# Attention and a feed-forward product on one core: later q and k loaded in 128-byte rows and transposed by VectorE, and the first block's weight operands requested by ScalarE

## The chip, the cores and the metric

One core of a Trainium2 chip. The time is device microseconds (us) of one execution, the median of several. The kernel before took 1540.1 us (three runs, 1538.55 to 1542.52; 1540.2 with a fourth, which ran beside the result); in the later series on two chips its medians were 1538.6 to 1539.1. "Faster" and "slower" mean by more than 2%. Ratios are the mean time of one kernel's runs over that of the kernel before's runs of the same rounds, so they are not quite the ratio of the medians that stand beside them. Stage lengths and waits come from one profiled run of each kernel.

## The reference, cut to what matters

```python
# q, k, v: (8, 12, 448, 64) float32;  w_in: (768, 2048), w_out: (2048, 768), both float64
q_n, k_n = rmsnorm(q, g_q), rmsnorm(k, g_k)          # over the 64 columns
attn = softmax(q_n @ k_n.T / 8)
x = (attn @ v) -> (8 * 448, 12 * 64)
h = maximum(x @ w_in, 0);  out = (h * h) @ w_out
```

Of the kernel before, what the change touches and what calls it, by code (L numbers as in the profile page):

```python
# [303 lines left out]
def load_pair(nc, qk, q, k, i):  # L304

    _, H, S, D = q.shape
    b, h0 = divmod(2 * i, H)
    for dst, src in ((qk[:, 0], q), (qk[:, 1], k)):
        nc.sync.dma_start(dst, src[b, h0:h0 + 2].rearrange("h (p j) d -> p h (j d)", j=4))
# [3 lines left out]
def attention_then_ffn_bounded(  # L313
# [48 lines left out]
    NSPAN = B // 2  # L362
    assert 2 * D == P and S % NJ == 0 and SP <= P and B % 2 == 0 and NPAIR % 2 == 0 and NFC % 2 == 0
# [4 lines left out]
    small = ctx.enter_context(tc.tile_pool(name="small", bufs=4))  # L368
# [8 lines left out]
    mhalf = consts.tile([SP, 2 * 2 * NJ], F32, name="mhalf")  # L377
    qk1 = consts.tile([SP, 2, 2, NJ * D], F32, name="qk1")
# [170 lines left out]
    def load_blocks(upto):  # L549

        while len(stream) < min(upto, NSPAN * (N1 + N2)):
            n = len(stream) % (N1 + N2)
            if written[0] < min(2 * (n // 7 + 1) if n < N1 else 2 * NFC, 2 * NFC):
                return
            sw = loads.tile([P, 4, P], F32, tag="sw", name="sw", bufs=5)
            if n < N1:
                sw = sw[:, 0:HC]
                src = w1s[n // 7, n % 7]
            else:
                n -= N1  # L560
                src = w2s[*uses2[n // (HF // 4)], n % (HF // 4)]
            nc.sync.dma_start(sw.rearrange("p c m -> p (c m)"), src)
            stream.append(sw)
# [5 lines left out]
    def load(i):  # L569
        qks[i] = (qk0, qk1)[i % 2]  # L570
        load_pair(nc, qks[i], q, k, i)

    def load_v(i):
        b, h0 = i // NPAIR, 2 * (i % NPAIR)
        vs[i] = loads.tile([SP, 2, NJ, D], F32, tag="vt", name="vt")
        nc.sync.dma_start(vs[i].rearrange("p h j d -> p h (j d)"),
                          v[b, h0:h0 + 2].rearrange("h (p j) d -> p h (j d)", j=NJ))

    def norm(i):
        qk = qks.pop(i)  # L580
        qkn = loads.tile([SP, 2, NJ, 2, D], F32, tag="qkn", name="qkn", bufs=2)
        sq = qkn.rearrange("p s j h d -> p (s j h d)")
        flat = qk.rearrange("p s h e -> p (s h e)")
        nc.scalar.activation(sq, flat, AF.Square)
# [4 lines left out]
        nc.gpsimd.tensor_tensor(rflat, rflat, mhalf, ALU.pow)  # L589
# [8 lines left out]
    def transposes(i, alone=False):  # L598
        qkn = normed.pop(i)
        if alone:  # L600
            pts[i] = [ps_m.tile([P, S], F32, tag="m", name="pt") for _ in range(2)]
        else:
            pt = ps_s.tile([P, 2, 512], F32, tag="s", name="pts")
            pts[i] = [pt[:, s, 0:S] for s in range(2)]
        for s, pt in enumerate(pts[i]):
            for j in range(NJ):
                nc.tensor.transpose(pt[:, j * SP:(j + 1) * SP],  # L607
                                    qkn[:, s, j].rearrange("p h d -> p (h d)"), ident[:SP, :SP])

    def take_transposes(i):  # L610
        qkTs[i] = loads.tile([P, 2, S], F32, tag="qkT", name="qkT")
        for s, pt in enumerate(pts.pop(i)):
            nc.scalar.activation(qkTs[i][:, s], pt, AF.Copy, scale=gains[:, s:s + 1])  # L613
# [37 lines left out]
    def finish(work, i):  # L651

        b, hp = divmod(i, NPAIR)
        rec = work.tile([P, S], F32, tag="rec", name="rec", bufs=1)
        nc.vector.reciprocal(rec, tots.pop(i))  # L655
        nc.vector.tensor_tensor(xT[:, b % 2, hp].rearrange("d (p j) -> d j p", j=NJ),
                                pavs.pop(i).rearrange("d (j p) -> d j p", j=NJ),
                                rec.rearrange("d (j p) -> d j p", j=NJ), ALU.mult)
        del vs[i]
# [15 lines left out]
    def attention(work, first, end, alone):  # L675


        last = (first // (2 * NPAIR) + 1) * 2 * NPAIR
        for i in range(first, end):
            if i + 3 < min(last + 2, B * NPAIR):  # L680
                load(i + 3)
            scores(work, i, 0, alone)
            scores(work, i, 1, alone)
            if i + 2 < last:
                norm(i + 2)
# [6 lines left out]
            if alone and i + 1 < last:  # L692
                transposes(i + 1, True)
            scores(work, i, 2, alone)
            scores(work, i, 3, alone)
            if alone:
                if i + 1 < last:
                    take_transposes(i + 1)
                yield
            values(i, alone)  # L700
            finish(work, i)
            if i == end - 1:
                combine_x(i)
            if not alone:
                if i + 1 < last:
                    transposes(i + 1)
                    take_transposes(i + 1)
# [142 lines left out]
    nc.vector.tensor_scalar(gains[:, 0:1], gains[:, 0:1], float(D) ** -0.5, None, ALU.mult)  # L850

    ALONE = 2

    def start_of(span):
        return 2 * span * NPAIR

    def ahead(u, nxt):
# [6 lines left out]
        if u == 7 * (HF - 1):  # L864
            transposes(nxt)
            take_transposes(nxt)

    with tc.tile_pool(name="words", bufs=2) as spare["pool"]:
# [5 lines left out]
        transposes(0, True)  # L874
# [4 lines left out]
        with tc.tile_pool(name="first_product", bufs=2, reuse_waits="tile") as work:  # L879
            for u, _ in enumerate(first_product(work, 0)):  # L880
                weights(EARLY + (LATE - EARLY) * (u + 1) // N1)
                ahead(u, start_of(1))
        with tc.tile_pool(name="alone", bufs=2, reuse_waits="tile") as work:
            for u, _ in enumerate(attention(work, start_of(1), start_of(1) + ALONE, True)):
                weights(LATE + (ALL - LATE) * (u + 1) // ALONE)
# [23 lines left out]
def kernel(  # L909
# [22 lines left out]
    qk0 = bound.tile([q.shape[2] // 4, 2, 2, 4 * D], F32, name="qk0")  # L932
# [48 lines left out]
```

## The kernel before: the parts that the change and the argument touch

Work goes by **head pairs** (two heads of a batch, 48 pairs) and by **spans** (two batches, 12 pairs, four spans). "Span" in this sense is a block of work; the span of a profile is the whole execution. The products are done by a seven-product scheme on half blocks; its weight operands are prepared on the chip in span 0 from the float64 words, written to device memory (`w1s`, `w2s`) and streamed back as `sw`. The order of the stages is: attention of span 0 with the weights' preparation beside it; first product of span 0 (the rest of the preparation beside it); two **lone pairs** (12 and 13) of span 1; then **mixed stages**, in which attention of the next span and the second product of the present one take turns on TensorE (PE), with first products of the later spans between them.

```python
def norm(i):                                  # one pair: 112 partitions x (q,k) x 2 heads x 4 rows x 64
    nc.scalar.activation(sq, flat, AF.Square)
    nc.vector.tensor_reduce(rflat, sq..., ALU.add)
    nc.vector.tensor_scalar(rflat, rflat, 1.0 / D, 1e-6, ALU.mult, ALU.add)
    nc.gpsimd.tensor_tensor(rflat, rflat, mhalf, ALU.pow)             # 16 columns
    for s in range(2):
        nc.gpsimd.tensor_tensor(qkn[:, s]..., qk[:, s]..., rstd..., ALU.mult)

def transposes(i, alone=False):               # PE, 8 per pair, into PSUM
    ...
            nc.tensor.transpose(pt[:, j * SP:(j + 1) * SP], qkn[:, s, j]..., ident[:SP, :SP])

def take_transposes(i):
    for s, pt in enumerate(pts.pop(i)):
        nc.scalar.activation(qkTs[i][:, s], pt, AF.Copy, scale=gains[:, s:s + 1])

def scores(work, i, c, pe_sums): ...          # sc = k.T q on PE; pr = exp(sc) on ScalarE; acc += pr on VectorE
def values(i, pe_sums): ...                   # pav = v.T pr on PE, then tot = ones.T acc on PE
def finish(work, i):
    nc.vector.reciprocal(rec, tots.pop(i))
    nc.vector.tensor_tensor(xT[...], pavs.pop(i)..., rec..., ALU.mult)

def attention(work, first, end, alone):       # alone: no second product beside it
    for i in range(first, end):
        ...load(i + 3); scores(i, 0); scores(i, 1); norm(i + 2)
        if not alone: yield                   # here the second product gets its turn
        ...scores(i, 2); scores(i, 3)
        if alone: ...; yield                  # here the weights' preparation gets its turn
        values(i, alone)
        finish(work, i)
        if not alone:
            if i + 1 < last:
                transposes(i + 1)
                take_transposes(i + 1)
            yield

def load_blocks(upto):                        # weight operands, five buffers
    ...
            nc.sync.dma_start(sw.rearrange("p c m -> p (c m)"), src)
```

## Time and profile before

| | before |
|---|---|
| median | 1540.1 us |
| span of the profiled run | 1535.9 us |
| PE busy | 1466.5 us, 95% |
| granted PE clock | 0.991 |
| PE starts the first product of span 0 | 157.2 us |
| PE starts the lone pairs | 311.7 us |
| PE starts the second product | 345.2 us |

The page's first part gives each engine's busy time and number of instructions; its second part cuts the span into 40 slices and gives busy tenths per slice. A group line reads: line of the kernel, engine, operation, output<-inputs, shapes, count | busy us, mean ns of one | idle us just before, with what ended it. A timeline line reads: start, duration, engine, line, operation, and in brackets how long the engine had been idle and what released it. A line of the waits reads: who waited <- for whom: us in total, times, longest. The lines themselves stand in the prediction.

### The profile page before, as it was taken

To read this page: it belongs to the slowest core of one execution; us is meant where nothing else is said; L and a number is where in the kernel's file an instruction comes from. 1 tells how busy PE (TensorE), PEld (TensorE's weight loads), DVE (VectorE), ACT (ScalarE), POOL (GpSimd) and SP (SyncE) were. 2 spreads that over 40 slices of the span, in tenths; PEclk is the share of its full clock that TensorE was granted. 3 is DMA by queue.
4 is the path that set the end of the run, shared out by engine and by line. 5 is a ranking of instruction groups with operands and counts; after the bars stand their busy time and mean duration, and the time that the engine had idled before them with its cause. 6 is when DMAs were issued, how large, how long until landed. Compare 5 with 4: busy or idle time off the path is not lost.

```text
span 1535.9 us, 14184 instructions
## 1 busy us (share of the span) xinstructions
PE 1466.5 (95%) x4968; PEld 681.0 (44%) x4968; DVE 808.5 (53%) x922; ACT 453.7 (30%) x622; POOL 517.4 (34%) x367
## 2 busy tenths in 40 slices
PE   5989888879999999999999999999999999999998
PEld 2433443424444445544444445554444445555554
DVE  3779987865765533345556642345556662332111
ACT  4766555542322201223322211123322221111000
POOL 4788567771322002433333102243333301221000
PEclk9999999999999999999999999999999999999999
DMA  5376786842333332333333333233324223333353
GB/s 160 96 212 191 256 287 228 276 146 79 96 90 103 91 93 87 88 115 97 72 102 89 89 86 97 88 100 92 96 83 104 71 71 99 88 88 101 102 112 74
DMA packets 224532, 180.36 MB, mean 117 GB/s; under 512 B 99012, under 2 KB 200900, under 8 KB 224452
## 3 DMA queue, kind: packets, MB, share of 16 engines
q1 hardware_dynamic: 224452, 179.36, 41.2%
q8 instruction: 42, 0.69, 0.2%
q14 instruction: 38, 0.31, 0.1%
HBM read 146.28 MB, written 33.03 MB: 117 GB/s over the span
## 4 chain that ended last, share of the span: by engine, by line
PE 74%; POOL 10%; DVE 7%; issue 5%; DMA 2%; ACT 1%; SPq 0%; POOLq 0%; DVEq 0%
PE ps L809 34%; PE pc L733 8%; PE pd L733 8%; PE pa L733 7%; PE sc L621 7%; DVE acc L629 5%; PE pb L733 4%; POOL rstd L589 3%; PE pav L638 3%; PE tot L649 2%; POOL qkn L591 2%; POOL gC L471 2%; PE pts L607 2%; POOL gC L478 1%; ACT pr L624 1%
## 5 line engine op out<-in xcount | busy, mean ns | idle before, releaser
L809 PE MATMUL ps<-gT,sw 128*128 128x448 f32 x768 | 302.2, 544 | 10.0 <-DMA sw<-w2s 10.0
L589 POOL TENSOR_TENSOR rstd<-rstd,mhalf 112x16 f32<-112x16 f32 x48 | 152.1, 3168 | 398.8 <-DVE rstd L588 398.8
L741 POOL TENSOR_TENSOR gT<-gT 128x448 f32<-128x448 f32 x112 | 112.9, 1008 | 454.5 <-ACT gT L737 454.0
L624 ACT ACTIVATE pr<-sc 112x896 f32<-112x896 f32 x192 | 166.1, 915 | 332.1 <-PE sc L621 331.8
L809 PE MATMUL ps<-gC,sw 128*128 128x448 f32 x576 | 227.1, 543 | 0.0
L809 PEld LDWEIGHTS ps<-gT,sw 128*128 128x128 f32 x768 | 143.6, 191 | 151.9 <-issue 140.5
L655 DVE RECIPROCAL rec<-tot 128x448 f32<-128x448 f32 x48 | 142.0, 2957 | 72.9 <-PE tot L649 72.9
L621 PE MATMUL sc<-qkT 64*112 64x448 f32 x768 | 172.6, 569 | 2.6 <-ACT qkT L613 1.6
L638 PE MATMUL pav<-pr,vt 112*64 112x448 f32 x768 | 163.1, 547 | 3.4 <-DMA vt<-in_v_dram 3.1
L733 PE MATMUL pa<-xT,sw 128*128 128x448 f32 x384 | 155.5, 541 | 0.2 <-DMA sw<-w1s 0.2
L809 PEld LDWEIGHTS ps<-gC,sw 128*128 128x128 f32 x576 | 106.9, 190 | 108.2 <-issue 105.5
L737 ACT ACTIVATE gT<-gT 128x448 f32<-128x448 f32 x96 | 55.2, 575 | 298.4 <-DVE gT L767 183.3
L629 DVE TENSOR_TENSOR acc<-acc,pr 112x896 f32<-112x896 f32 x68 | 96.8, 1423 | 86.9 <-ACT pr L624 83.3
L591 POOL TENSOR_TENSOR qkn<-qk,rstd 112x512 f32<-112x512 f32 x96 | 120.5, 1276 | 3.8
L621 PEld LDWEIGHTS sc<-qkT 64*112 64x112 f32 x768 | 61.9, 175 | 98.6 <-issue 90.0
L733 PEld LDWEIGHTS pa<-xT,sw 128*128 128x128 f32 x384 | 73.1, 191 | 73.1 <-issue 72.0
L638 PEld LDWEIGHTS pav<-pr,vt 112*64 112x64 f32 x768 | 51.7, 137 | 102.7 <-issue 84.0
L629 DVE TENSOR_TENSOR acc<-pr 112x896 f32<-112x896 f32 x34 | 37.1, 1091 | 102.9 <-ACT pr L624 102.9
L733 PE MATMUL pc<-xC,sw 128*128 128x448 f32 x192 | 79.2, 549 | 5.4 <-DMA sw<-w1s 5.4
L733 PE MATMUL pd<-xT,sw 128*128 128x448 f32 x192 | 79.1, 549 | 4.7 <-DVE z L756 4.7
L733 PE MATMUL pd<-xC,sw 128*128 128x448 f32 x192 | 77.8, 541 | 5.3 <-DVE gT L767 4.2
L733 PE MATMUL pb<-xC,sw 128*128 128x448 f32 x192 | 77.8, 540 | 3.3 <-DVE gC L483 1.6
(82 smaller groups left out, 1404.8 us busy)
## 6 DMA issues: line engine op xcount, KB each, us to landing
sw<-w1s SPq DMA_DIRECT2D x224, 192.0 KB, 2.4
sw<-w2s SPq DMA_DIRECT2D x168, 256.0 KB, 2.7
qk<-in_q_dram SPq DMA_DIRECT2D x48, 224.0 KB, 3.3
qk<-in_k_dram SPq DMA_DIRECT2D x48, 224.0 KB, 3.7
vt<-in_v_dram SPq DMA_DIRECT2D x48, 224.0 KB, 3.7
w1s<-gC SPq DMA_DIRECT2D x8, 1344.0 KB, 6.0
w2s<-gC SPq DMA_DIRECT2D x24, 448.0 KB, 3.7
out_dram<-osb SPq DMA_DIRECT2D x192, 56.0 KB, 1.9
```

The lines of the kernel that those rows point to most:

```text
L471: nc.gpsimd.tensor_tensor(b[to[n % 2][half]], f[:, part], e[:, part], ALU.mult)
L589: nc.gpsimd.tensor_tensor(rflat, rflat, mhalf, ALU.pow)
L591: nc.gpsimd.tensor_tensor(qkn[:, s].rearrange("p j h d -> p h j d"), qk[:, s].rearrange("p h (j d) -> p h j d", d=D), rstd[:, s].rearrange ...
L621: nc.tensor.matmul(sc[:, h, 0:S], qkT[rows, 1, c * SP:(c + 1) * SP], qkT[rows, 0, :], start=True, stop=True)
L624: nc.scalar.activation(pr, sc[:, :, 0:S], AF.Exp)
L629: nc.vector.tensor_tensor(accs[i], probs[i, 0] if c == 1 else accs[i], pr, ALU.add)
L638: nc.tensor.matmul(pavs[i][h * D:(h + 1) * D, :], vs[i][:, h, c, :], pr[:, h, :], start=(c == 0), stop=(c == NJ - 1))
L655: nc.vector.reciprocal(rec, tots.pop(i))
L733: nc.tensor.matmul(ps, stream[n][:, c], rhs[:, c], start=first and c == 0, stop=c == HC - 1, skip_group_check=not first)
L737: nc.scalar.activation(g, src, AF.Relu)
L741: nc.gpsimd.tensor_tensor(g, g, g, ALU.mult)
L809: nc.tensor.matmul(ps, stream[n][:, c % 4], rhs_of[i][:, c], start=c == 0, stop=c == HF - 1)
```

## The change

Its intent: take 272 transposes off PE, which is the bound from 345 us on. From pair 14 on (`NAT = 14`), q and k are loaded so that partition `32 n + t` holds quarter `n` of the pair's 128 columns of rows `t`, `t + 32`, ...; VectorE's transpose of 32x32 squares then gives the layout that the scores need. The price is rows of 128 bytes, 28 sums per partition where there were 16, and an exchange of half sums between neighbouring quarters. The gain of k is folded into that of q, and v of these pairs is loaded in the matching order, by two loads instead of one (left out of the cut below). Beside it, span 0's weight operands go to ScalarE's queue; norms 12 and 13 and the transposes of pair 12 move from the first product of span 0 into the attention before it; and the last weights are all prepared in the first lone pair.

```diff
+    ALONE = 2
+    NAT = 2 * NPAIR + ALONE
...
-            nc.sync.dma_start(sw.rearrange("p c m -> p (c m)"), src)
+            queue = nc.scalar if len(stream) < N1 else nc.sync
+            queue.dma_start(sw.rearrange("p c m -> p (c m)"), src)
...
     def load(i):
+        if i < NAT: (as before)
+        for s, src in enumerate((q, k)):
+            dst = by_squares(qks[i])[:, s]
+            for n in range(4):
+                nc.sync.dma_start(dst[n * 32:(n + 1) * 32],
+                                  src[b, h0 + n // 2, :, n % 2 * 32:n % 2 * 32 + 32]
+                                  .rearrange("(g t) e -> t g e", t=32))
...
+    def norm_by_squares(i):
+        nc.scalar.activation(qkn..., qk..., AF.Square)
+        nc.vector.tensor_reduce(half, qkn..., AX, ALU.add)              # 128x28
+        for n in range(4):
+            m = n ^ 1
+            nc.vector.tensor_copy(other[n * 32:(n + 1) * 32], half[m * 32:(m + 1) * 32])
+        nc.vector.tensor_tensor(half, half, other, ALU.add)
+        nc.vector.tensor_scalar(half, half, 1.0 / D, 1e-6, ALU.mult, ALU.add)
+        nc.gpsimd.tensor_tensor(half, half, mhalf, ALU.pow)             # 28 columns
+        for s in range(2):
+            nc.gpsimd.tensor_tensor(qkn[:, s], qk[:, s], half..., ALU.mult)
...
     def transposes(i):
+        if i >= NAT:
+            for s in range(2):
+                nc.vector.transpose(qkTs[i][:, s], qkn[:, s].rearrange("p g e -> p (g e)"))
+            nc.scalar.activation(qkTs[i][:, 0], qkTs[i][:, 0], AF.Copy, scale=gains[:, 0:1])
+            return
...
     def finish(work, i):
+        (from NAT on) nc.vector.tensor_tensor(xT[:, b % 2, hp], pavs.pop(i), rec, ALU.mult)
...
     def attention(work, first, end, alone):
-        last = (first // (2 * NPAIR) + 1) * 2 * NPAIR
+        last = NAT if alone else (first // (2 * NPAIR) + 1) * 2 * NPAIR
...
-            if i + 2 < last:
+            if i + 2 < (start_of(2) if alone else last):
                 norm(i + 2)
...
             values(i, alone)
             finish(work, i)
+            if i + 1 == NAT or not alone and i + 1 < last:
+                transposes(i + 1)
...
             for u, _ in enumerate(first_product(work, 0)):
                 weights(EARLY + (LATE - EARLY) * (u + 1) // N1)
-                ahead(u, start_of(1))
...
             for u, _ in enumerate(attention(work, start_of(1), start_of(1) + ALONE, True)):
-                weights(LATE + (ALL - LATE) * (u + 1) // ALONE)
+                weights(ALL)
```

More of the change, by code (lines that the diff above doesn't have):

```diff
@@ L307, in load_pair @@
     b, h0 = divmod(2 * i, H)
+    qk = qk[:S // 4].rearrange("p (s h e) -> p s h e", s=2, h=2)
     for dst, src in ((qk[:, 0], q), (qk[:, 1], k)):
@@ L362, in attention_then_ffn_bounded, with start_of @@
     NSPAN = B // 2
+    ALONE = 2
+    NAT = 2 * NPAIR + ALONE
+    def start_of(span):
+        return 2 * span * NPAIR
     assert 2 * D == P and S % NJ == 0 and SP <= P and B % 2 == 0 and NPAIR % 2 == 0 and NFC % 2 == 0
@@ L367, in attention_then_ffn_bounded @@
     loads = ctx.enter_context(tc.tile_pool(name="loads", bufs=2))
-    small = ctx.enter_context(tc.tile_pool(name="small", bufs=4))
+    small = ctx.enter_context(tc.tile_pool(name="small", bufs=2))
     dram = ctx.enter_context(tc.tile_pool(name="dram", bufs=1, space=bass.MemoryType.DRAM))
@@ L376, in attention_then_ffn_bounded @@
     gains = consts.tile([P, 2], F32, name="gains")
-    mhalf = consts.tile([SP, 2 * 2 * NJ], F32, name="mhalf")
-    qk1 = consts.tile([SP, 2, 2, NJ * D], F32, name="qk1")
+    mhalf = consts.tile([P, 2 * (S // 32)], F32, name="mhalf")
+    qk1 = consts.tile([P, 2 * 2 * NJ * D], F32, name="qk1")
     gT = consts.tile([P, NFC, 2 * S], F32, name="gT")
@@ L570, in load, with by_squares @@
         qks[i] = (qk0, qk1)[i % 2]
-        load_pair(nc, qks[i], q, k, i)
+        if i < NAT:
+            load_pair(nc, qks[i], q, k, i)
+            return
+        b, h0 = i // NPAIR, 2 * (i % NPAIR)
+        for s, src in enumerate((q, k)):
[4 more added lines that the diff above has]
+                                  .rearrange("(g t) e -> t g e", t=32))
+    def by_squares(flat):
+        return flat[:, 0:2 * S].rearrange("p (s g e) -> p s g e", s=2, e=32)
     def load_v(i):
@@ L575, in load_v @@
         vs[i] = loads.tile([SP, 2, NJ, D], F32, tag="vt", name="vt")
-        nc.sync.dma_start(vs[i].rearrange("p h j d -> p h (j d)"),
-                          v[b, h0:h0 + 2].rearrange("h (p j) d -> p h (j d)", j=NJ))
-    def norm(i):
-        qk = qks.pop(i)
-        qkn = loads.tile([SP, 2, NJ, 2, D], F32, tag="qkn", name="qkn", bufs=2)
-        sq = qkn.rearrange("p s j h d -> p (s j h d)")
-        flat = qk.rearrange("p s h e -> p (s h e)")
-        nc.scalar.activation(sq, flat, AF.Square)
+        if i < NAT:
+            nc.sync.dma_start(vs[i].rearrange("p h j d -> p h (j d)"),
+                              v[b, h0:h0 + 2].rearrange("h (p j) d -> p h (j d)", j=NJ))
+        else:
+            for h in range(2):
+                nc.sync.dma_start(vs[i][:, h], v[b, h0 + h].rearrange("(j p) d -> p j d", j=NJ))
+    def norm(i):
+        if i >= NAT:
+            return norm_by_squares(i)
+        qk = qks.pop(i)[:SP].rearrange("p (s h e) -> p s h e", s=2, h=2)
+        flat_n = loads.tile([P, 4 * P * 2], F32, tag="qkn", name="qkn", bufs=2)
+        qkn = flat_n[:SP].rearrange("p (s j h d) -> p s j h d", s=2, j=NJ, h=2)
+        sq = flat_n[:SP]
+        nc.scalar.activation(sq, qk.rearrange("p s h e -> p (s h e)"), AF.Square)
         rstd = small.tile([SP, 2, 2, NJ], F32, tag="rstd", name="rstd")
@@ L588, in norm @@
         nc.vector.tensor_scalar(rflat, rflat, 1.0 / D, 1e-6, ALU.mult, ALU.add)
-        nc.gpsimd.tensor_tensor(rflat, rflat, mhalf, ALU.pow)
+        nc.gpsimd.tensor_tensor(rflat, rflat, mhalf[:SP, 0:4 * NJ], ALU.pow)
         for s in range(2):
@@ L596, in norm, with transposes @@
         normed[i] = qkn
-    def transposes(i, alone=False):
-        qkn = normed.pop(i)
-        if alone:
-            pts[i] = [ps_m.tile([P, S], F32, tag="m", name="pt") for _ in range(2)]
-        else:
-            pt = ps_s.tile([P, 2, 512], F32, tag="s", name="pts")
-            pts[i] = [pt[:, s, 0:S] for s in range(2)]
+    def norm_by_squares(i):
+        qk = by_squares(qks.pop(i))
+        qkn = by_squares(loads.tile([P, 4 * P * 2], F32, tag="qkn", name="qkn", bufs=2))
+        NG = S // 32
+        nc.scalar.activation(qkn.rearrange("p s g e -> p (s g e)"), qk.rearrange("p s g e -> p (s g e)"), AF.Square)
+        half = small.tile([P, 2 * NG], F32, tag="half", name="half")
+        other = small.tile([P, 2 * NG], F32, tag="other", name="other")
+        nc.vector.tensor_reduce(half, qkn.rearrange("p s g e -> p (s g) e"), AX, ALU.add)
+        for n in range(4):
[5 more added lines that the diff above has]
+        for s in range(2):
+            nc.gpsimd.tensor_tensor(
+                qkn[:, s], qk[:, s],
+                half[:, s * NG:(s + 1) * NG].rearrange("p g -> p g ()").to_broadcast([P, NG, 32]), ALU.mult)
+        normed[i] = qkn
+    def transposes(i):
+        qkn = normed.pop(i)
+        if i >= NAT:
+            qkTs[i] = loads.tile([P, 2, S], F32, tag="qkT", name="qkT")
+            for s in range(2):
+                nc.vector.transpose(qkTs[i][:, s], qkn[:, s].rearrange("p g e -> p (g e)"))
+            nc.scalar.activation(qkTs[i][:, 0], qkTs[i][:, 0], AF.Copy, scale=gains[:, 0:1])
+            return
+        pts[i] = [ps_m.tile([P, S], F32, tag="m", name="pt") for _ in range(2)]
         for s, pt in enumerate(pts[i]):
@@ L610, in take_transposes @@
     def take_transposes(i):
-        qkTs[i] = loads.tile([P, 2, S], F32, tag="qkT", name="qkT")
-        for s, pt in enumerate(pts.pop(i)):
-            nc.scalar.activation(qkTs[i][:, s], pt, AF.Copy, scale=gains[:, s:s + 1])
+        if i < NAT:
+            qkTs[i] = loads.tile([P, 2, S], F32, tag="qkT", name="qkT")
+            qT, kT = pts.pop(i)
+            nc.scalar.activation(qkTs[i][:, 0], qT, AF.Copy, scale=gains[:, 0:1])
+            nc.scalar.copy(qkTs[i][:, 1], kT)
     def scores(work, i, c, pe_sums):
@@ L655, in finish @@
         nc.vector.reciprocal(rec, tots.pop(i))
-        nc.vector.tensor_tensor(xT[:, b % 2, hp].rearrange("d (p j) -> d j p", j=NJ),
-                                pavs.pop(i).rearrange("d (j p) -> d j p", j=NJ),
-                                rec.rearrange("d (j p) -> d j p", j=NJ), ALU.mult)
+        if i < NAT:
+            nc.vector.tensor_tensor(xT[:, b % 2, hp].rearrange("d (p j) -> d j p", j=NJ),
+                                    pavs.pop(i).rearrange("d (j p) -> d j p", j=NJ),
+                                    rec.rearrange("d (j p) -> d j p", j=NJ), ALU.mult)
+        else:
+            nc.vector.tensor_tensor(xT[:, b % 2, hp], pavs.pop(i), rec, ALU.mult)
         del vs[i]
@@ L675, in attention @@
     def attention(work, first, end, alone):
-        last = (first // (2 * NPAIR) + 1) * 2 * NPAIR
+        last = NAT if alone else (first // (2 * NPAIR) + 1) * 2 * NPAIR
         for i in range(first, end):
-            if i + 3 < min(last + 2, B * NPAIR):
+            if i + 3 < (NAT + 3 if alone else min(last + 2, B * NPAIR)):
                 load(i + 3)
@@ L691, in attention @@
                 load_v(i + 1)
-            if alone and i + 1 < last:
-                transposes(i + 1, True)
+            if alone and i + 1 < NAT:
+                transposes(i + 1)
             scores(work, i, 2, alone)
@@ L696, in attention @@
             if alone:
-                if i + 1 < last:
-                    take_transposes(i + 1)
+                take_transposes(i + 1)
                 yield
@@ L703, in attention @@
                 combine_x(i)
+            if i + 1 == NAT or not alone and i + 1 < last:
+                transposes(i + 1)
             if not alone:
-                if i + 1 < last:
-                    transposes(i + 1)
-                    take_transposes(i + 1)
                 yield
@@ L849, in attention_then_ffn_bounded @@
     norm(0)
-    nc.vector.tensor_scalar(gains[:, 0:1], gains[:, 0:1], float(D) ** -0.5, None, ALU.mult)
-    ALONE = 2
-    def start_of(span):
-        return 2 * span * NPAIR
+    nc.vector.tensor_scalar(gains[:, 0:1], gains[:, 0:1], gains[:, 1:2], float(D) ** -0.5, ALU.mult, ALU.mult)
     def ahead(u, nxt):
@@ L865, in ahead @@
             transposes(nxt)
-            take_transposes(nxt)
     with tc.tile_pool(name="words", bufs=2) as spare["pool"]:
@@ L873, in attention_then_ffn_bounded @@
         norm(1)
-        transposes(0, True)
+        transposes(0)
         take_transposes(0)
@@ L931 @@
     top = bound.tile([1, 1], F32, name="top")
-    qk0 = bound.tile([q.shape[2] // 4, 2, 2, 4 * D], F32, name="qk0")
+    qk0 = bound.tile([128, 16 * D], F32, name="qk0")
     load_pair(nc, qk0, q, k, 0)
```

## The prediction

> **What bounds the kernel now.** I read the page first: the busy totals, then the 40 slices. Each slice is 38.4 us (1535.9 / 40).
>
> ```profile
> PE 1466.5 (95%) x4968; PEld 681.0 (44%) x4968; DVE 808.5 (53%) x922; ACT 453.7 (30%) x622; POOL 517.4 (34%) x367
> PE   5989888879999999999999999999999999999998
> DVE  3779987865765533345556642345556662332111
> POOL 4788567771322002433333102243333301221000
> ```
>
> From slice 9 on (345 us), PE is at 9 tenths: there, time falls only if matmul work goes away. The first 345 us ("span 0": attention alone, first product, two more pairs of attention) hold some 54 of PE's 69 idle us (windows of 100 us: 18.5, 8.4, 15.5 and 11.6 us idle), with POOL and DVE at 7 to 9 tenths. So there are two regimes, and the change has a part for each. The groups of instructions, split by shape, say what the PE transposes cost and what their replacements are like:
>
> ```profile
> L607 PE MATMUL pts<-ident,qkn 112*128 112x112 f32 x272 | 33.3, 265 | 0.0
> L613 ACT ACTIVATE qkT<-pts,gains 128x448 f32<-128x448 f32 x68 | 39.4, 630 | 133.3 <-PE pts L607 133.3
> L798 DVE STREAM_TRANSPOSE osb<-ct 128x448 f32<-128x448 f32 x48 | 30.6, 636 | 0.6
> L589 POOL TENSOR_TENSOR rstd<-rstd,mhalf 112x16 f32<-112x16 f32 x48 | 152.1, 3168 | 398.8 <-DVE rstd L588 398.8
> ```
>
> The 272 transposes belong to 34 head pairs (8 each), exactly the pairs from 14 on that the change reroutes. The timeline of one pair in the late stage (start, duration; PE lines, then DVE lines) shows what one set occupies:
>
> ```profile
> 861.86 0.97 PE L649 MATMUL tot<-acc,ones 112*64 112x448 f32 x4
> 862.77 0.98 PE L607 MATMUL pts<-ident,qkn 112*128 112x112 f32 x8
> 863.59 0.93 PE L809 MATMUL ps<-gC,sw 128*128 128x448 f32 x2
> 864.36 3.92 PE L809 MATMUL ps<-gT,sw 128*128 128x448 f32 x10
> 868.21 1.76 PE L621 MATMUL sc<-qkT 64*112 64x448 f32 x8
> ...
> 862.91 2.96 DVE L655 RECIPROCAL rec<-tot 128x448 f32<-128x448 f32 x1 [1.10 <-PE tot L649]
> 865.90 0.96 DVE L656 TENSOR_TENSOR xT<-pav,rec 128x448 f32<-128x448 f32 x1
> ```
>
> The reader is to see two things: the transposes hold PE from 862.77 to 863.59, 0.82 us, and after them PE has 4.62 us of second product (12 instructions) until the next pair's scores.
>
> **What the Trainium skill says.** "TensorE: Matmul & The Clock Gate", Part 4, says that a PE transpose lands in PSUM and needs a copy after it: the trace agrees (two ScalarE copies of 0.63 us per pair). "VectorE: DVE Perf Modes", The three transpose paths, says that VectorE transposes only blocks of 32x32, into SBUF; that is why the loads change layout, and L798 shows 0.636 us for 128x448. "SBUF — State Buffer", Who interferes with whom, says that a VectorE instruction with two SBUF inputs contends with a GpSimd instruction that reads SBUF. The trace agrees for the multiplications of the norm: the two acc additions take 3.76 us beside them and 2.29 without.
>
> ```profile
> 763.53 2.90 POOL L589 TENSOR_TENSOR rstd<-rstd,mhalf 112x16 f32<-112x16 f32 x1 [13.45 <-DVE rstd L588]
> 766.51 2.89 POOL L591 TENSOR_TENSOR qkn<-qk,rstd 112x512 f32<-112x512 f32 x2
> 766.59 3.76 DVE L629 TENSOR_TENSOR acc<-acc,pr 112x896 f32<-112x896 f32 x2 [1.98 <-ACT pr L624]
> 877.36 2.29 DVE L629 TENSOR_TENSOR acc<-acc,pr 112x896 f32<-112x896 f32 x2 [2.99 <-ACT pr L624]
> ```
>
> The power (L589) seems not to block VectorE: at 328.44 one ran beside two-input subtractions that kept their 0.51 us each, and itself stretched to 3.61. "DMA: Bandwidth & Descriptors", Issuing engines are not separate DMA queues, says that SP's and ScalarE's DMAs share 16 engines and interleave, and only issue time is saved; its section on queues gives each its own rings. No run yet shows rings of both.
>
> **The change, part by part, pairs 14 to 47.**
> PE loses 34 x 0.82 = 27.9 us, all of it in stages where PE is the bound. That is the ceiling of this part.
> ScalarE: two copies (2 x 0.63) become one scaling of q in SBUF; like L737's 0.575 us, so 0.7 us less per pair.
> VectorE gains two transposes (2 x 0.636), four small copies and one addition (estimate 0.6 us, from the 0.17 of L588); the sum over 896 instead of 1024 columns saves 0.15 of 1.22, the unpermuted xT some 0.35 of 0.98 (L756, the same shapes unpermuted, takes 0.618). Net some 1.4 us per pair of 18.5 us, in which VectorE is now busy 55 to 60%: capacity is there.
> GpSimd: the power runs over 28 columns, not 16: 2.90 x 28/16 = 5.1 us; the multiplications shrink by 1/8. The norm takes 7 us in place of 5, one pair ahead of need: hidden. But the multiplications start 3 us later, at the reciprocal (one PSUM input) and no longer beside acc. PE's waits for acc (tot <- acc, 7.7 us in all, 15 times) should mostly go: 7 us gained.
> What moves onto the path: the next scores now need VectorE to do reciprocal, xT, two transposes in this order after tot. From the start of the reciprocal: 2.99 + 0.56 + 0.57 + 0.64 = 4.76 us (0.57 is the pitch at which such instructions follow each other), and ScalarE's scaling of q ends at about 4.8; scores at 5.0 after PE could begin its second-product pieces. PE has 10, 12, 14 or 16 instructions there, at 0.378 us: 3.8, 4.5, 5.3, 6.0. From the chain in order of time, span 1 has 14 to 17 (no stall), the two later stages 14 three times, 12 six times, 10 twice. With 0.2 us for the exposed weight load, stalls are 0, 0.7 and 1.4: 7 us per stage, 14 us in all.
> DMA: q and k of a pair become 8 DMAs of 448 rows of 128 bytes. The output tiles are just such DMAs: four at the end (1792 rows) were issued in 1.91 us and filled 1.58 us of the 16 engines. So one pair's loads cost some 4 us of SP and 3 to 4 us of the engines (estimate; reads may be dearer than these writes), of 18.5 us, with DMA at 0.35. Operands sw are fetched four blocks ahead (4 x 3.15 us at least). I expect this hidden.
> Sum: 27.9 + 7 - 14 = 21 us.
>
> **Span 0.** Lines of the waits, the chain and SP's timeline:
>
> ```profile
> PE ps L809 <- DMA sw<-w2s: 10.0, 1, 10.0
> 209.10 7.17 DMA sw<-w1s
> 208.03 0.37 SPq L514 DMA_DIRECT2D w1s<-gC  x1
> 208.50 0.51 SPq L448 DMA_DIRECT2D gT<-in_moe_w_out_dram  x1
> 209.10 3.02 SPq L562 DMA_DIRECT2D sw<-w1s  x3
> ```
>
> An operand sat behind a 1344 KB write and a 768 KB load of the same queue, 7.17 us, and PE waited. On ScalarE's queue it is issued as soon as its buffer is free. PE's waits for sw in the first product are 8.7 us; with what they drag along (VectorE waits, slower clock after the gaps) I take 9 to 10 us gained. ScalarE pays 56 issues of about 0.35 us, 20 us beside a stage where it is 55% busy.
> Norms of pairs 12 and 13 and a set of transposes move from the first product into the attention before it, where GpSimd paces the pairs (11.6 us each): +4 us. In return GpSimd has 10 us less in the first product, and all remaining weights are prepared ahead of norm 15. The 10.0 us wait for the last weights then vanishes, but scores of pair 14 come right behind reciprocal, xT and transposes of the pair before, with no PE work between: 5 us stall there. Sum: 10 - 4 + 5 = 11 us.
>
> Total 21 + 11 = 32 us: 1540.1 - 32 = 1508.
>
> **The rivals.**
> (1) VectorE's late transposes take back everything: if the chain is 1 us longer than reckoned, most of 34 pairs stall by it and the first part is worth nothing; 1529. For it: reciprocal is on the chain, VectorE is in order. Against: span 1's pieces cover it.
> (2) Small rows: if a 128-byte read costs several times the 14 ns x 16 engines of the output rows, the loads delay sw and the norms, and the time stands or rises, 1535 to 1560. Against: the outputs' rows move at 105 to 120 GB/s; DMA is two thirds idle.
> (3) Nothing stalls: full 27.9 + 7 and up to 20 us in span 0; 1487.
> (4) ScalarE in order with waits for PE's buffers before its evacuations delays the first product: span 0 gains nothing; 1518.
>
> **Range and chances.** The line for 2% faster is 1509.3, just at my value; stalls (0 to 28 us) and span 0 (0 to 20 us) carry the width. 1493 to 1526; faster 0.52, same 0.46, slower 0.02.
>
> **What would show it.** Right: no L607 group for pts; PE's second-product and score counts unchanged; a new wait of scores for DVE or ACT qkT, 0.5 to 1.5 us, some 16 times and none in span 1; acc additions near 1.1 us; power near 5.1 us; sw waits in the first product under 2 us; no 10 us wait for w2s but some 5 us before pair 14. Wrong: PE waits for sw or qk in the late stages, SP busy with qk for over 6 us a pair, acc blocked by the longer power, or a first product that is no shorter than before (154 us).

## The result, and the profile after

The changed kernel took 1514.3 us (four runs, 1510.31 to 1516.42) beside 1540.2 us of the kernel before; the ratio is 0.983 with an interval of 0.980 to 0.985: 1.7% faster, which is under the 2%. In a later series, five runs gave 1513.9 and 0.9835 (0.982 to 0.985). Both outputs are correct. 1514.3 lies in the stated range, 6 us above the stated 1508.

The page of the changed kernel, and its groups that took the place of those shown before:

```profile
PE 1443.2 (95%) x4696; PEld 658.8 (44%) x4696; DVE 828.4 (55%) x1160; ACT 431.4 (29%) x588; POOL 554.9 (37%) x367
PE   5998889888999999999999999999999999999998
...
L653 DVE STREAM_TRANSPOSE qkT<-qkn 128x448 f32<-128x448 f32 x68 | 39.4, 617 | 0.0
L654 ACT ACTIVATE qkT<-qkT,gains 128x448 f32<-128x448 f32 x34 | 22.7, 668 | 238.5 <-DVE qkT L653 238.5
L640 POOL TENSOR_TENSOR half<-half,mhalf 128x28 f32<-128x28 f32 x34 | 166.2, 4888 | 316.7 <-DVE half L639 262.5 <-DMA qk<-in_q_dram 33.1 <-DMA sw<-w2s 21.2
```

PE has 272 instructions less and is still at 95%: what was taken from it came off the time where it was the bound. The 68 VectorE transposes take 0.617 us each (0.636 reckoned), the power 4.89 us (5.1 reckoned). But the slice from 113 us has fallen to 8 tenths while the one before it has risen to 9, and the slices from 150 to 380 us do not look better than before. Where the stages begin in PE's timeline (and, from 530 us on, in the chain in order of time) says it in numbers:

| stage | before, us | changed, us | difference | predicted |
|---|---|---|---|---|
| up to the first product of span 0 | 157.2 | 163.8 | +6.6 | +4 |
| first product of span 0 | 154.5 | 147.8 | -6.7 | -10 |
| lone pairs, up to the second product | 33.5 | 38.9 | +5.4 | -5 |
| mixed stage of span 0, to its last pair | 193.2 | 183.7 | -9.5 | |
| the same point one span later | 360.1 | 350.1 | -10.1 | -21 for these three |
| and one more | 359.3 | 349.3 | -10.0 | |
| the rest | 278.1 | 278.4 | +0.3 | 0 |

The late stages gained 29.5 us, more than the 21 predicted; span 0 lost 5.3 us where a gain of 11 was predicted. Both differences have to be explained.

First the late stages. The timeline of one pair of the changed kernel (PE lines, then VectorE lines, then GpSimd lines):

```profile
709.14 0.92 PE L703 MATMUL tot<-acc,ones 112*64 112x448 f32 x4
709.99 4.03 PE L864 MATMUL ps<-gT,sw 128*128 128x448 f32 x10
715.03 1.76 PE L675 MATMUL sc<-qkT 64*112 64x448 f32 x8 [1.02 <-ACT qkT L654]
...
706.46 2.29 DVE L683 TENSOR_TENSOR acc<-acc,pr 112x896 f32<-112x896 f32 x2 [2.46 <-ACT pr L678]
710.11 2.96 DVE L709 RECIPROCAL rec<-tot 128x448 f32<-128x448 f32 x1 [1.36 <-PE tot L703]
713.10 0.62 DVE L715 TENSOR_TENSOR xT<-pav,rec 128x448 f32<-128x448 f32 x1
713.64 1.16 DVE L653 STREAM_TRANSPOSE qkT<-qkn 128x448 f32<-128x448 f32 x2
...
703.55 4.79 POOL L640 TENSOR_TENSOR half<-half,mhalf 128x28 f32<-128x28 f32 x1 [8.89 <-DVE half L639]
708.43 2.02 POOL L642 TENSOR_TENSOR qkn<-qk,half 128x448 f32<-128x448 f32 x2
```

The chain of the prediction stands there: reciprocal from 710.11, xT, transposes, ScalarE's scaling of q, scores at 715.03, which is 5.04 us after PE could begin its second-product pieces at 709.99 (reckoned: 5.0). PE had ten instructions for that time, which took 4.03 us (reckoned: 3.8), and stood still for 1.02 us. And the two acc additions take 2.29 us, because the multiplications now begin at 708.43, when acc is nearly done.

Now span 0. PE's two longest single waits after the kernel's start, and the timeline around them (VectorE, GpSimd, PE):

```profile
PE pav L692 <- DVE xT L711: 6.8, 1, 6.8
PE sc L675 <- ACT qkT L654: 12.5, 17, 5.2
```

```profile
319.23 4.80 POOL L640 TENSOR_TENSOR half<-half,mhalf 128x28 f32<-128x28 f32 x1 [1.45 <-DVE half L639]
328.04 1.03 DVE L486 TENSOR_TENSOR gC<-gC 128x384 f32<-128x384 f32 x2 [8.89 <-POOL gC L479]
328.99 2.95 DVE L709 RECIPROCAL rec<-tot 128x448 f32<-128x448 f32 x1
332.97 1.76 PE L692 MATMUL pav<-pr,vt 112*64 112x448 f32 x4 [6.84 <-DVE xT L711]
```

VectorE stood idle for 8.89 us in front of two subtractions of the weights (L486), which waited for GpSimd, which had the longer power to do first. The reciprocal of pair 12 is behind those subtractions in VectorE's order, and PE's pav of pair 13 is behind that reciprocal. Of the 17 waits of scores for qkT, one is 5.2 us long: the boundary before pair 14. The other 16 sum to 7.3 us.

### The profile page after: what moved, and what is told of

Read it like the earlier page. It is cut to its first block, busy times and chain, and to the rows that moved or that the text cites. A ratio compares the mean times of both kernels' runs of the same rounds, so it can differ in the third digit from the quotient of the medians.

```text
span 1512.0 us, 14222 instructions
## 1 busy us (share of the span) xinstructions
PE 1443.2 (95%) x4696; PEld 658.8 (44%) x4696; DVE 828.4 (55%) x1160; ACT 431.4 (29%) x588; POOL 554.9 (37%) x367
## 4 chain that ended last, share of the span: by engine, by line
PE 73%; POOL 9%; DVE 7%; issue 5%; DMA 4%; ACT 1%; SPq 0%; POOLq 0%; DVEq 0%; ACTq 0%
PE ps L864 30%; PE sc L675 8%; PE pa L788 8%; PE pav L692 7%; PE pc L788 7%; PE pd L788 7%; PE pb L788 4%; DVE rec L709 4%; POOL rstd L618 3%; POOL gC L479 2%; PE tot L703 2%; POOL qkn L620 2%; DMA sw<-w1s 2%; POOL gC L486 1%; DMA gC<-in_moe_w_out_dram 1%
## 5 line engine op out<-in xcount | busy, mean ns | idle before, releaser
L640 POOL TENSOR_TENSOR half<-half,mhalf 128x28 f32<-128x28 f32 x34 | 166.2, 4888 | 316.7 <-DVE half L639 262.5
L683 DVE TENSOR_TENSOR acc<-acc,pr 112x896 f32<-112x896 f32 x68 | 74.7, 1099 | 59.6 <-ACT pr L678 56.1
L654 ACT ACTIVATE qkT<-qkT,gains 128x448 f32<-128x448 f32 x34 | 22.7, 668 | 238.5 <-DVE qkT L653 238.5
L788 PE MATMUL pc<-xT,sw 128*128 128x448 f32 x192 | 77.5, 540 | 0.8 <-DMA sw<-w1s 0.8
```

Source lines behind the costliest of these rows:

```text
L640: nc.gpsimd.tensor_tensor(half, half, mhalf, ALU.pow)
L683: nc.vector.tensor_tensor(accs[i], probs[i, 0] if c == 1 else accs[i], pr, ALU.add)
L788: nc.tensor.matmul(ps, stream[n][:, c], rhs[:, c], start=first and c == 0, stop=c == HC - 1, skip_group_check=not first)
```

## The experiments

Each is told with its edit against the changed kernel unless said otherwise. Stage lengths are read as in the table above.

### The queue alone, and the queue taken back

Three runs. The first edit is on the kernel before, the second on the changed kernel; the second was run twice, the second time beside the unedited changed kernel.

```diff
 (on the kernel before)
-            nc.sync.dma_start(sw.rearrange("p c m -> p (c m)"), src)
+            queue = nc.scalar if len(stream) < N1 else nc.sync
+            queue.dma_start(sw.rearrange("p c m -> p (c m)"), src)
 (on the changed kernel)
-            queue = nc.scalar if len(stream) < N1 else nc.sync
+            queue = nc.sync
```

Queue alone, expected:

> The kernel before with only the queue part of the change. Theory: the first product falls by 5 to 8 us from 154.5 us, waits of PE for sw in it from 8.7 us to under 3 us, total 1532 to 1536 us. Rival: the first product is bound by VectorE and GpSimd preparing weights, or ScalarE in order holds the loads back: within 2 us of 1540.

Measured: 1543.6 us, ratio 1.002 (1.001 to 1.003; with the profiled run of 1550.4 us counted, the means give 1.003). The theory was wrong and the rival was right in direction, though its "within 2 us of 1540" was missed by 1.6: no gain, if anything a small loss. In its profiled run (the slowest of the five, by 6.4 us) the first product lasted 161.1 us, not 154.5. PE's waits for sw did fall, from 8.7 to 2.7 us, but its waits for VectorE's z rose from 4.7 to 15.9 us.

Queue taken back, expected the first time:

> The changed kernel with span 0's weight operands back on SyncE's queue. Theory: ScalarE's queue is what shortened the first product of span 0 (154.5 us before, 147.8 us changed), because operands no longer wait behind weight writes and word loads; without it the first product is 152 us or more and the time 1518 to 1523 us. Rival: the 6.7 us come from the two norms that left the first product; then the first product stays under 149 us and the time within 2 us of 1514.

Measured: 1516.4 us, ratio 0.985 (0.983 to 0.986); first product 145.2 us: the rival's side. Expected the second time, and for the changed kernel beside it:

> The changed kernel with span 0's weight operands on SyncE's queue, again, now beside the changed kernel itself. Theory after the first runs: the queue's part is worth little (0 to 3 us), since PE's waits for operands only turn into waits for VectorE: 1514 to 1518, under 3 us from the changed kernel. Rival: it is worth the 10 us of the prediction: 1522 or more.

> The changed kernel once more, unedited, to stand on the same chip and beside the same runs of the kernel before as the next three. Both theories: 1512 to 1517 us.

Measured: 1515.4 us (0.985, 0.983 to 0.986) against 1513.9 us (0.9835, 0.982 to 0.985). The queue is worth 1.5 us by these medians and 2.1 by those of the first time; the intervals overlap, so even that is not clear of the noise, and it is not 10. The first product lasts 147.0 us with SyncE's queue and 147.1 with ScalarE's. The longest waits of PE in and just before it say why. First with SyncE's queue, then with ScalarE's:

```profile
PE pa L788 <- DMA sw<-w1s: 12.4, 3, 9.0
PE pc L788 <- DMA sw<-w1s: 5.6, 3, 3.0
PE pd L788 <- DVE z L811: 0.8, 2, 0.6
PE pd L788 <- DVE gT L822: 0.3, 1, 0.3
```

```profile
PE pa L788 <- DMA sw<-w1s: 5.8, 2, 4.0
PE pc L788 <- DMA sw<-w1s: 1.6, 2, 0.9
PE pd L788 <- DVE z L811: 4.6, 4, 2.3
PE pd L788 <- DVE gT L822: 4.1, 3, 2.5
```

With the smaller lines counted that are not shown here, the waits for operands go down by 10 us (19.8 to 9.7) and those for VectorE up by 8 us (1.1 to 9.5). VectorE, 84 to 86% busy from 200 to 300 us in these runs and the changed kernel, is the next to be waited for in the first product, so a PE that comes sooner only waits for it. What remains is the first operand: it is waited for 9.0 us behind the small-row loads of pair 14 on SyncE's queue, and 4.0 us on ScalarE's.

### The norms back in the first product

The edit gives the attention of span 0 its old limits and calls `ahead(u, start_of(1))` in the first product again. With the two norms, the first small-row load (pair 14) and the transposes of pair 12 go back too, so the run tests them together. The diff is cut.

```diff
+        head = alone and first == 0
-        last = NAT if alone else ...
+        last = start_of(1) if head else NAT if alone else ...
...
                 weights(EARLY + (LATE - EARLY) * (u + 1) // N1)
+                ahead(u, start_of(1))
```

> The changed kernel with norms 12 and 13, load 14 and transposes 12 back in the first product of span 0, where the kernel before had them. Theory: the two norms held up GpSimd's weights in the attention before, and with them the write that the first operand load waits for; back in place the first product starts at 157 to 159 us, not 163.8, and is 2 to 5 us longer than 147.8: total 1509 to 1513. Rival: the moved work costs the same in either place: within 1.5 us of 1514.

Measured: 1520.2 us, ratio 0.988 (0.986 to 0.989). The theory's first half held (the first product starts at 159.0 us), its second half not: the first product lasts 159.7 us, 12 us more, with PE's waits for z at 11.7 us. So both my theory and its rival were wrong: on ScalarE's queue the move gained some 6 us. Of the 6.7 us by which the first product got shorter, the norms are the cause, not the queue (without them 147 us on either queue; with them 154.5 on SyncE's and 160 to 161 on ScalarE's). The norm's square sum stands in VectorE's order ahead of z and waits for ScalarE there, 4.2 to 4.3 us in all on either queue. What the two slow runs have beyond that shows in their traces: their longest wait for z (6.0 us with the queue alone, 5.5 us with the norms back) ends a stall of VectorE, 5.79 and 5.30 us, in front of one weight step that stands ahead of z; with the queue alone it waited there for a load of weight words. In the kernel before, the same step waited 0.41 us. Why it is late on ScalarE's queue was not isolated.

The moment at which PE starts the lone pairs adds up the attention and the first product, and shows how the two parts of the change go together:

| | SyncE's queue | ScalarE's queue |
|---|---|---|
| norms in the first product | 311.7 us (before) | 321.9 (queue alone), 318.7 (norms back) |
| norms in the attention | 313.1 and 314.1 (queue taken back, twice) | 311.6 and 311.1 (changed kernel, twice) |

Each part alone was no gain up to there, and both together only came back to where the kernel before had been. So the 6 us of the move hold beside ScalarE's queue; beside SyncE's no gain is seen. (In the lower row the attention also holds the first small-row loads; their share was not taken apart.)

### The last weights spread over both lone pairs

```diff
-                weights(ALL)
+                weights(LATE + (ALL - LATE) * (u + 1) // ALONE)
```

> The changed kernel with the last eight weight steps of span 0 spread over the two lone pairs again, as before. Theory: preparing all at once put two VectorE subtractions that wait for GpSimd (behind the 4.8 us power) ahead of the reciprocal of pair 12, and so made the 6.8 us wait of pav for xT; spread, that wait is under 1 us and matmuls there keep their 0.92 us. But the last weights are then written after norm 15, so PE waits 5 to 8 us for the first sw of w2s: net 1510 to 1513. Rival: having weights early is what counts; spread out costs 3 us or more: 1517 and up.

Measured: 1515.4 us, ratio 0.984 (0.983 to 0.985), no gain: above the 1510 to 1513 of the theory and below the 1517 of the rival. Each wait did about what was expected of it: that for xT fell from 6.8 to 0.3 us, and one of 8.4 us for the first operand of w2s took its place. The lone pairs lasted 37.9 us instead of 38.9. The order of the last weights changes which wait PE has, hardly how long.

### Pair 14 the old way

```diff
-    NAT = 2 * NPAIR + ALONE
+    NAT = 2 * NPAIR + ALONE + 1
```

> The changed kernel with one more pair (14) loaded and transposed the old way. Theory: the boundary between span 0 and the mixed stage loses its 5.2 us wait of scores for qkT, the power of norm 14 is 2.9 and not 4.8 us so the 6.8 us wait of pav for xT falls to 4 to 5 us, PE pays 0.8 us for 8 transposes; the first operands of w2s may then be waited for by some 3 us: net 1508 to 1512. Rival: the boundary is set by when the last weights are written, not by the transposes: within 1.5 us of the changed kernel.

Measured: 1509.8 us, ratio 0.9815 (0.980 to 0.983), in the expected range: the 5.2 us wait is gone, that for xT is 3.8 us, the wait for w2s is 6.0 us (twice what was expected), and the lone pairs last 34.35 us, 4.6 us less.

### VectorE's transposes ahead of the reciprocal

```diff
             scores(work, i, 3, alone)
+            if i + 1 == NAT or not alone and i + 1 < last:
+                transposes(i + 1)
...
             finish(work, i)
-            if i + 1 == NAT or not alone and i + 1 < last:
-                transposes(i + 1)
```

> The changed kernel with VectorE's transposes of the next pair issued right after the last scores of a pair, ahead of its reciprocal, so that the next scores no longer wait for reciprocal, xT, transposes, scaling. Theory: the 16 stalls of the late stages (7.3 us) go, and the 5.2 us before pair 14 shrink, though there PE may then wait up to 4 us for the first operands of w2s: 1502 to 1507 us, no wait of scores for ACT qkT over 0.3 us in the late stages. Rival: the transposes ahead of the reciprocal delay it and with it xT and the second product's additions, so PE waits elsewhere: 1512 or more.

Measured: 1505.0 us, ratio 0.978 (0.977 to 0.979), faster than the kernel before by over 2%. The same pair, VectorE and then PE:

```profile
710.28 1.16 DVE L653 STREAM_TRANSPOSE qkT<-qkn 128x448 f32<-128x448 f32 x2
711.73 2.96 DVE L709 RECIPROCAL rec<-tot 128x448 f32<-128x448 f32 x1 [0.28 <-PE tot L703]
...
715.57 1.76 PE L675 MATMUL sc<-qkT 64*112 64x448 f32 x8
```

The transposes fit between the acc additions and the end of tot, where VectorE had idled 1.36 us; the reciprocal still waits for tot (0.28 us), and the scores wait for nothing. The last two of the three late stages are 345.9 and 345.1 us, 4.2 us each below the changed kernel. That is the stall, shown by taking it away. At the boundary, PE now waits 6.2 us for w2s (up to 4 were expected) in place of the 5.2 us for qkT.

### The power over 16 columns only

Only 16 of 28 columns are raised to the power, so that the power lasts as long as before the change and the multiplications start 2 us earlier.

```diff
-        nc.gpsimd.tensor_tensor(half, half, mhalf, ALU.pow)
+        nc.gpsimd.tensor_tensor(half[:, 0:16], half[:, 0:16], mhalf[:, 0:16], ALU.pow)
```

> The changed kernel with the power over 16 of its 28 columns (a wrong result on purpose; the values stay near 1): the power takes 2.9 us again, so that the norm's multiplications start 2 us sooner. Theory: the acc additions became short (1.42 to 1.10 us) only because the longer power moved the multiplications from beside them to beside the reciprocal; with the short power acc is 1.3 us or more again, waits of tot for acc return (3 to 8 us in all) and the late stages are up to 5 us longer, against 1 to 3 us gained in span 0: 1512 to 1519. Rival: acc is short for another reason (shape or place of the multiplications): acc stays at 1.10 and the time falls or stays, 1508 to 1514.

Measured: 1520.8 us, ratio 0.988 (0.987 to 0.990), outputs wrong; the theory's side, though above its 1512 to 1519. Less work on GpSimd made the kernel slower. The power took 2.99 us, acc went from 1.10 to 1.32 us on average, waits of tot for acc are back (3.1 us seen as idle PE), and the three late stages are 187.7, 352.4 and 351.6 us: 4.0, 2.3 and 2.3 us longer. One pair's VectorE and GpSimd lines:

```profile
396.60 3.30 DVE L683 TENSOR_TENSOR acc<-acc,pr 112x896 f32<-112x896 f32 x2
...
396.26 2.69 POOL L642 TENSOR_TENSOR qkn<-qk,half 128x448 f32<-128x448 f32 x2
```

The two additions take 3.30 us beside the multiplications, 2.29 without. So some 8.6 us of the late stages' gain come from the longer power, by its timing alone. The way there is only in part seen. PE's idle time accounts for 3.1 us. The weight loads of tot, which the profile lists apart from PE, waited 9.9 us for acc in the changed kernel, 25.0 us in this run and 29.7 us in the kernel before; that fits, but how much of these waits PE pays was not measured.

### The small-row loads twice

Each of the eight loads is issued a second time into a scratch in device memory.

```diff
                 nc.sync.dma_start(dst[n * 32:(n + 1) * 32], src[b, h0 + n // 2, ...]...)
+                nc.sync.dma_start(again[s, n * 32:(n + 1) * 32]..., src[b, h0 + n // 2, ...]...)
```

> The changed kernel with every 128-byte-row load of q and k issued a second time, into a scratch in device memory that nobody reads: 16 such DMAs per pair in place of 8. Theory: the small rows are hidden; with twice as many, the late stages stay within 1 us each of 183.7, 350.1 and 349.3 us and only span 0's end (where SyncE's queue holds these loads ahead of the first w2s operands) grows, by 4 to 10 us: 1518 to 1525. Rival: small rows cost time now, so doubling them costs at least as much again in the late stages: 1535 or more, with waits of PE for sw there.

Measured: 1533.6 us, ratio 0.997 (0.995 to 0.998), above the range that I gave. The mixed stage of span 0 is 184.5 us (+0.8) and the late stages 352.1 and 352.4 us (+2.0 and +3.1), two to three times what the theory allowed; one wait of PE for w1s in each, 1.7 and 2.9 us, in the later first products accounts for that. Such waits in the late stages were the rival's sign, and the time is near its 1535, so the rival was partly right. The lone pairs grow from 38.9 to 47.8 us, with 8.1 us of waiting for w2s. So one set of loads is hidden in the mixed stages, but by no wide margin in the first products, and at the end of span 0 SyncE's queue has no room for more. A second copy is not the first one taken away: what the first costs at that end is not measured by this run.

### A version that beats both

The transposes ahead of the reciprocal, pair 14 the old way, the last two subtractions of the weights on GpSimd, and the first five w2s operands requested right behind the last weight writes.

```diff
-        late = t >= EARLY // 4
+        late = EARLY // 4 <= t < 2 * NFC + 2
...
                 weights(ALL)
+                load_blocks(N1 + 5)
```

> A version meant to beat both: the changed kernel with VectorE's transposes ahead of the reciprocal, pair 14 the old way, the last two weight subtractions on GpSimd so that VectorE's reciprocal of pair 12 waits for nobody, and the first five w2s operands requested right behind the last weight writes, ahead of the small-row loads. Theory: late stages as in the run with transposes first (about 346 and 345 us), no wait of pav for xT in the lone pairs, first second-product matmul at 336 to 342 us: 1493 to 1499. Rival: the end of span 0 is bound by the weights' chain on GpSimd, and the extra GpSimd work moves it back: 1500 or more.

Measured: 1497.4 us (1492.9 to 1500.0), ratio 0.972 (0.971 to 0.974), correct: 2.8% faster than the kernel before. Of its four parts, the first two have runs of their own above; the other two were not tried apart. The second product starts at 340.8 us instead of 350.5, after lone pairs of 26.2 us. The wait for xT is gone, and PE's pav of pair 13 runs at its usual pace:

```profile
330.14 0.97 PE L692 MATMUL pav<-pr,vt 112*64 112x448 f32 x4
...
340.78 4.59 PE L864 MATMUL ps<-gT,sw 128*128 128x448 f32 x7 [2.72 <-DMA sw<-w2s]
```

The same with the operands requested one pair later (`if u == 1:` ahead of `load_blocks`):

> The same, but the five operands requested one pair later, behind load 16 and ahead of load 17. Theory: SyncE issues them some 6 us later, so PE waits for them 2 to 6 us more than in the version before; load 16 lands earlier instead: 1496 to 1503. Rival: load 16 is the later of the two needs, and this one is the faster.

Measured: 1499.0 us, ratio 0.974 (0.973 to 0.975), with a wait for w2s of 7.8 us instead of 2.7. The medians differ by 1.6 us in the expected direction, but the intervals overlap.

## Why the prediction was right or wrong, point by point

- **The time.** 1508 was said, 1514.3 came, inside the range. The chances leaned slightly to "faster by over 2%" (0.52 against 0.46); it came out at 1.7%. That the sum was near is luck: two errors of opposite sign met, 8.5 us too little for the late stages and 16 us too much for span 0.
- **The ceiling of 27.9 us** (34 x 0.82) is in keeping with the stages: the late two spans lost 12 sets each, 9.8 us, and gained 10.1 and 10.0 us net. But the 272 transposes of the group that was read are not "exactly the pairs from 14 on": they are those of pair 12 (at 294.8 us) and of pairs 15 to 47. Pair 14's stood in the lone pairs, under another tile name. Where PE is the bound, 33 sets went, 27.1 us; that the number 34 came out is a coincidence.
- **The stalls that take its place.** The mechanism was right to the instruction: reciprocal, xT, transposes, scaling, 5.04 us where 5.0 was reckoned, 16 waits where 16 were said, none in span 1's covered pieces. The size was off: "7 us per stage, 14 us in all" measured 7.3 us in all, mean 0.46 us. The pieces in front of it last longer than reckoned (ten instructions 4.03 us, not 3.8; twelve 4.78, not 4.5), and the "0.2 us for the exposed weight load" does not show as idle time: behind twelve PE waited 0.26 to 0.29 us and not 0.7, behind ten 1.02 and not 1.4. Taking the stall away gave 8.4 us in the two late stages.
- **The acc additions.** "7 us gained" from the later multiplications: the experiment with the short power measured 8.6 us. That the later start gains it is shown; that all of it goes through PE's waits for acc, as the prediction has it, is not.
- **Together,** 27.1 + 8.6 - 7.3 = 28.4, or 27.3 with the 8.4 us that taking the stall away gave, against 29.5 measured; 1 to 2 us are not assigned. The term that was mis-sized is the stall.
- **Small rows.** "I expect this hidden" held in the mixed stages: a set of eight loads was issued in 3.9 us there (some 4 us estimated). In span 0 it did not: beside a weight write and a word load, the first set took SyncE 9.0 us.
- **"I take 9 to 10 us gained"** from ScalarE's queue: this step failed. It is worth 1.5 to 2 us at most in the changed kernel and nothing in the kernel before. I counted waits of PE for operands as time, though VectorE was nearly as late; they turned into waits for VectorE (10 us less of the one, 8 us more of the other). Rival (4) had this outcome ("span 0 gains nothing"), for a reason that no run here tests. Why the queue alone makes the first product longer is not settled.
- **"+4 us" for the moved norms** was 6.6: 2.6 us in the attention and 4.0 us of waiting for the first operand. That they leave the first product by 7 us shorter I had put down to the queue. Beside ScalarE's queue their move is a gain of some 6 us, which the prediction had as a loss. Up to the lone pairs the queue and the move were to gain 6 us together; they gained under 1.
- **"The 10.0 us wait for the last weights then vanishes"** held, and so did the "5 us stall" before pair 14 (5.2). What the step missed: with all weights prepared at once, VectorE's subtractions wait for GpSimd behind the longer power, and the reciprocal of pair 12 waits behind them: 6.8 us. After the two gaps PE also ran slower: four pav took 1.76 us instead of 0.97, eight sc 3.33 instead of 1.76; the granted clock from 312 to 352 us was 0.79, against 0.87 before and 0.96 in the best version. It was 1.00 from 312 to 326 us, 0.52 from 332 to 339 behind the first gap, 0.91 from 339 to 347 and 0.50 from 347 to 351 behind the second. The Trainium skill ("TensorE: Matmul & The Clock Gate", Part 1) says that the clock's default is throttled and that activity releases it; by these numbers the trace agrees. So the stage came out at +5.4 instead of -5, the largest single miss.

## What to carry to other kernels

Work moved off the bound engine pays only if its new place is early enough in the other engine's order: here the same two VectorE instructions, moved from behind a reciprocal to ahead of it, gave 8.4 us over two stages. A wait that the profile shows is worth its length only if nothing else would have been waited for at the same moment; look at the busy share of the second in line before counting it. And in an in-order engine, an instruction that waits for a slower engine holds back everything behind it, so place such instructions where nothing urgent follows.

## What the Trainium skill lacked or had wrong

- "SBUF — State Buffer", Who interferes with whom, calls contention for the port pair that VectorE and GpSimd share an exclusive lock: whoever issues first has it for the whole instruction, and the other is blocked. By that a VectorE addition of two SBUF inputs should wait for a GpSimd power that reads SBUF. A power of 4.79 us (from 703.55) did not hold up acc additions that began at 706.46 and took the usual 2.29 us. Beside GpSimd's multiplications, both sides slowed (acc 2.29 to 3.30 us for two, the multiplications 1.84 to 2.69).
- No page was found with the cost of a power on GpSimd: where nothing slowed it, 2.90 us for 16 columns, over 112 as over 128 partitions, and 4.79 for 28 over 128, so about 0.17 to 0.18 us a column.
- "DMA: Bandwidth & Descriptors", Issuing engines are not separate DMA queues, says that a second issuing engine saves only issue time, usually small. It was not small here: the first weight operand was waited for 9.0 us on the queue that also issued eight small-row loads (8.5 to 9.0 us of issue beside large transfers, 3.9 us in a quiet stage) and 4.0 us on the other. In the kernel's time it still came to 1.5 to 2 us at most.
- "TensorE: Matmul & The Clock Gate", Part 4, gives some 275 ns for a transpose (128x128, bf16) in one kernel's context. Single transposes (112x112, float32) show 0.265 us here, but eight in a row occupied PE for only 0.82 us, about 0.10 us each.
